# LSH attention and two gated MLPs on one core: code rows, a clamping maximum pass, bursts of value products, and single banks for the last outputs

## The chip, the cores and the metric

The kernel runs on one core of a Trainium2 chip. The metric is device microseconds of one execution, the median of several runs. Engines are named as the profile names them: PE (TensorE; PEld is its weight load), DVE (VectorE), ACT (ScalarE), POOL (GpSimd), SP (SyncE, which here only issues transfers).

## The reference

Attention of 2 batches x 8 heads, 768 positions, 64 features, in which a query sees only the keys of its own bucket; the bucket is the pattern of six signs. Two MLPs follow, 1536 tokens, width 512, inner width 2048, with outputs of their own gate each. All weights of the MLPs arrive as float64.

```python
q_bucket = sum(((q @ proj) > 0) * 2**arange(6))      # keys likewise
scores = where(q_bucket == k_bucket, q @ k.T / sqrt(64), -1e9)
attn = exp(scores - max); attn = attn / (attn.sum() + 1e-9)
x = (attn @ v) as [1536, 512]
h = x @ w_in;  x = (h - tanh(h)) @ w_out             # first MLP
h = x @ w_in2; out = (h * sigmoid(1.702 * h)) @ w_out2
```

## The kernel before

**Attention.** Heads go in eight pairs `i`. The work is a loop over 96 steps `s`: a step is 128 queries of one head against all 768 keys, twelve steps to a pair, six to a unit `u` (384 queries of both heads). In the loop, step `s` issues, in this order on PE:

- `scores(s + 2)`: two products of 128 rows each, into a score tile of two PSUM banks (tag S, two tiles). The first product has the high and low parts of q in `qa` against k doubled in `ka`; the second has q's high part and the bucket mask in `qb` against k's low part and the mask in `kb`. Rows 0 to 63 of `kb` and `qb` hold features, rows 64 to 127 the 64 buckets: a one in the key's bucket in `kb`, and -2^100 in all buckets but the query's in `qb`.
- `pv(u, c)`: one of six key chunks of the value products of the unit before, one product per head, each with half of PE's columns.
- `transposes(s)`: six 128x128 transposes of the probabilities into two banks (tag T), copied to `probT` by ACT (L377); in steps 20, 22, 44 and 46 by DVE.
- at one step of a unit, `spread`: three transposes of the inverse row sums (`rb`, L413).

`softmax` has DVE take the row maximum of the score tile (L348) and scale it (L350); ACT then takes exp from the score tile to `pr` in SBUF, with row sums (L352). The score tile comes free when exp has read it. `finish` multiplies the value products by the inverse sums (DVE) and has POOL split them into `xh` and `xl` for the MLPs.

**Preparing a pair.** `prep_ahead` runs while the pair before is worked on. At that pair's step 1 (step 3 for pair 1), POOL computes the low parts (`split_q` L238, `split_k` L244), PE the sign products (`prep_bits`, L262) and DVE their comparison with 0 (L271). At four later steps (`PO`), `prep_hot` has PE turn the bits into sums per bucket (`po`, L293), from which DVE makes the two mask blocks (L305, L308). The first scores of the new pair are issued nine steps after step 1 (seven for pair 1). The kernel does pair 0 in another way, in pieces, with ACT in it. SP's queue carries `r`, `v` and the raw weights; POOL's queue carries `ka`, `qa`, `qb`, and once `sel` (256 KB), the table of L293.

**MLPs.** 16 chunks of two inner blocks. Their work is issued in an order written by hand as a string of names (`STEADY`, and `ORDER` for single chunks): `h` and `P` are products in, `t`, `g`, `hi`, `lo` the gate and its split, `o` the products out (`out_mm`, token block t, inner block j, feature block d), `ev` the addition of the result (`evac`, L711, on DVE). A suffix - means the chunk before. Output tiles are halves of two-bank S tiles. After the last chunk an `ORDER` of its own ends the program, and each `ev` of the last chunk issues the output transfer of its block.

The scheduler is manual: the order of the code is the order on each engine, and waits are set by the tiles.

Of the kernel before, what the change touches and what calls it, by code (L numbers as in the profile page):

```python
# [57 lines left out]
def lsh_attention_then_two_mlps(  # L58
# [193 lines left out]
    def prep_bits(i, hs=(0, 1), tag="g"):  # L252
        r = heads[i][4]
        pb = ps.tile([128, 512], F32, tag=tag, name=f"pb{i}_{hs[0]}")
        if hs[0] == 0:
# [14 lines left out]
        rows = slice(hs[0] * 64, hs[-1] * 64 + 64)  # L270
        nc.vector.tensor_scalar(bits[i][rows], pb[rows, :HALF], 0.0, None, op0=ALU.is_gt)  # L271

    def prep_hot(i, h, f, tag="g"):
# [1 line left out]
        c = slice(f * HALF, (f + 1) * HALF)  # L280
# [1 line left out]
        po = ps.tile([128, 512], F32, tag=tag, name=f"po{i}_{h}_{f}")
        if i == 0:
            nc.tensor.matmul(
                po[:, :HALF],
                sel0[g : g + 32],
                bits[i][g : g + 32],
                start=True,
                stop=True,
                tile_position=(g, 0),  # L290
            )
        else:
            nc.tensor.matmul(po[:, :HALF], sel_sb[:, g // 32], bits[i], start=True, stop=True)  # L293

        def masks():
            if i == 0:
                nc.scalar.activation(
                    kb[64:128, h, c], po[64:128, :HALF], AF.Relu, bias=hot_sb[64:128], scale=BIG
                )
                nc.vector.tensor_scalar(  # L300
                    qb[64:128, h, c], po[0:64, :HALF], pop_sb[0:64], -1.0,
                    op0=ALU.subtract, op1=ALU.max,
                )
                return
            nc.vector.tensor_scalar(  # L305
                kb[64:128, h, c], po[64:128, :HALF], pop_sb[64:128], None, op0=ALU.is_equal
            )
# [51 lines left out]
    def transposes(s, on_vector):  # L359
# [5 lines left out]
        for a in range(2):  # L365
# [8 lines left out]
            if on_vector:  # L374
                copies.append((dst, src))
            else:
                nc.scalar.activation(dst, src, AF.Copy)  # L377
# [558 lines left out]
```

## Time and profile before

| | us |
|---|---|
| median of 3 runs (771.14 to 772.78) | 771.51 |
| profiled execution | 772.15 |
| its span | 770.0 |
| PE, DVE, ACT, POOL busy | 749.5, 585.1, 424.3, 400.6 |
| PE busy with `sc` (two groups), `tp`, `pv` | 55.7 + 50.2, 83.5, 82.0 |
| PE busy with `po` | 11.8 |

The span is the time between the first and the last record of the profiled execution; the rest of its own time lies around it. Busy time of PE is the union of its matmuls, which overlap, so the sum over groups is more than the union. An "idle before" names the engine whose event ended the idle time.

### The profile page before, as it was taken

To read this page: it belongs to the slowest core of one execution; us is meant where nothing else is said; L and a number is where in the kernel's file an instruction comes from. 1 tells how busy PE (TensorE), PEld (TensorE's weight loads), DVE (VectorE), ACT (ScalarE), POOL (GpSimd) and SP (SyncE) were. 2 spreads that over 40 slices of the span, in tenths; PEclk is the share of its full clock that TensorE was granted. 3 is DMA by queue.
4 is the path that set the end of the run, shared out by engine and by line. 5 is a ranking of instruction groups with operands and counts; after the bars stand their busy time and mean duration, and the time that the engine had idled before them with its cause. 6 is when DMAs were issued, how large, how long until landed. Compare 5 with 4: busy or idle time off the path is not lost.

```text
span 770.0 us, 10036 instructions
## 1 busy us (share of the span) xinstructions
PE 749.5 (97%) x3708; PEld 570.0 (74%) x3708; DVE 585.1 (76%) x840; ACT 424.3 (55%) x793; POOL 400.6 (52%) x342
## 2 busy tenths in 40 slices
PE   5899999999999999999999999999999999999996
PEld 3566666666666688888888888887888888888885
DVE  4778778767667768878887787897798778877653
ACT  3777777777778466354353543656545355353430
POOL 6451651643410586564644745699774474564620
PEclk9999999999999999999999999999999999999999
DMA  9535234043120211131112111302022211130004
GB/s 266 177 104 192 88 104 163 22 145 125 40 76 1 110 55 66 45 110 54 55 66 83 72 55 54 110 6 104 24 87 78 81 60 55 55 110 0 1 11 154
DMA packets 12993, 62.89 MB, mean 82 GB/s; under 512 B 1616, under 2 KB 2512, under 8 KB 8848
## 3 DMA queue, kind: packets, MB, share of 16 engines
q1 hardware_dynamic: 8928, 46.21, 16.7%
q0 software_dynamic: 3872, 15.99, 7.1%
q8 instruction: 29, 0.48, 0.3%
q14 instruction: 20, 0.16, 0.1%
q10 hardware_dynamic: 144, 0.05, 0.0%
HBM read 59.10 MB, written 3.15 MB: 81 GB/s over the span
## 4 chain that ended last, share of the span: by engine, by line
PE 88%; DVE 3%; POOL 2%; issue 2%; DMA 2%; ACT 1%; POOLq 0%; DVEq 0%; ACTq 0%
PE o L703 31%; PE h L614 12%; PE y L614 10%; PE pv L388 10%; PE tp L369 9%; PE sc L334 8%; PE w L614 5%; PE x L614 2%; DMA r<-in_rr 1%; DMA ka<-in_kd 1%; POOL xl L726 1%; PE rb L413 1%; PE pb L262 1%; PE po L293 1%; DVE acc L594 1%
## 5 line engine op out<-in xcount | busy, mean ns | idle before, releaser
L676 POOL TENSOR_TENSOR gl<-f,gh 128x512 fp32r<-128x512 f32 x62 | 86.2, 1390 | 162.1 <-ACT gh L671 156.7
L711 DVE TENSOR_TENSOR acc<-o,acc 128x512 f32<-128x512 f32 x168 | 108.6, 684 | 48.6 <-PE o L703 48.1
L377 ACT ACTIVATE pt<-tp 128x384 f32<-128x384 f32 x184 | 80.3, 489 | 47.9 <-PE tp L369 47.0
L348 DVE TENSOR_REDUCE nm<-sc 128x1 f32<-128x768 f32 x96 | 91.6, 954 | 14.6 <-PE sc L334 13.4
L369 PEld LDWEIGHTS tp<-eye_sb,pr 128*128 128x128 f32 x576 | 61.6, 140 | 53.5 <-issue 25.7
L145 POOL TENSOR_TENSOR wl<-w,wh 128x512 fp32r<-128x512 f32 (+1 forms) x62 | 86.4, 1405 | 19.0 <-ACT wh L142 18.9
L352 ACT ACTIVATE pr<-sc,nb 128x768 f32<-128x768 f32 x96 | 87.0, 906 | 16.0 <-DVE nb L350 8.9
L369 PE MATMUL tp<-eye_sb,pr 128*128 128x128 f32 x576 | 83.5, 281 | 0.0
L388 PE MATMUL pv<-pt,v 128*64 128x384 f32 x384 | 82.0, 510 | 0.0
L735 ACT ACTIVATE u<-y 128x512 f32<-128x512 f32 x42 | 25.2, 600 | 100.6 <-PE y L614 100.6
L703 PE MATMUL o<-wh,gh 128*128 128x512 f32 x192 | 75.0, 391 | 0.9 <-ACT acc L709 0.7
L703 PE MATMUL o<-wh,gl 128*128 128x512 f32 x192 | 74.8, 390 | 0.5 <-POOL gl L676 0.5
L703 PE MATMUL o<-gh,wh 128*128 128x512 f32 x192 | 74.8, 390 | 0.0
L703 PE MATMUL o<-wl,gh 128*128 128x512 f32 x192 | 74.7, 389 | 0.0
L703 PE MATMUL o<-gl,wh 128*128 128x512 f32 x192 | 74.7, 389 | 0.0
L703 PE MATMUL o<-gh,wl 128*128 128x512 f32 x192 | 74.7, 389 | 0.0
L614 PE MATMUL h<-xl,wh 128*128 128x512 f32 x160 | 62.4, 390 | 0.6 <-POOL xl L726 0.6
L614 PE MATMUL h<-xh,wh 128*128 128x512 f32 x160 | 62.4, 390 | 0.0
L614 PE MATMUL h<-xh,wl 128*128 128x512 f32 x160 | 62.3, 389 | 0.0
L334 PE MATMUL sc<-ka,qa 128*128 128x384 f32 x192 | 55.7, 371 | 2.3 <-DVE qa L238 1.9
L671 ACT ACTIVATE gh<-f 128x512 fp32r<-128x512 f32 x62 | 39.0, 629 | 28.7 <-DVE f L667 28.5
L334 PE MATMUL sc<-kb,qb 128*128 128x384 f32 x192 | 50.2, 342 | 2.0 <-DVE qb L300 2.0
(138 smaller groups left out, 1652.7 us busy)
## 6 DMA issues: line engine op xcount, KB each, us to landing
raw<-in_w SPq DMA_DIRECT2D x32, 1024.0 KB, 4.8
ka<-in_kd POOLq DMA_DIRECT2D x7, 768.0 KB, 4.7
qa<-in_qd POOLq DMA_DIRECT2D x7, 768.0 KB, 6.7
r<-in_rr SPq DMA_DIRECT2D x7, 768.0 KB, 4.5
v<-in_vv SPq DMA_DIRECT2D x8, 384.0 KB, 3.1
out<-acc SPq DMA_DIRECT2D x12, 256.0 KB, 2.1
qb<-in_qd POOLq DMA_DIRECT2D x7, 384.0 KB, 8.0
r<-in_rr SPq DMA_DIRECT2D x2, 384.0 KB, 4.2
```

The source lines that it names most:

```text
L145: nc.gpsimd.tensor_tensor(wl[c, j][:, f], ws[c, j][:, f], wh[c, j][:, f].bitcast(F32), ALU.subtract)
L334: nc.tensor.matmul(sc[:, hf, :HALF], (qa, qb)[n][:, h, t0 : t0 + QT], (ka, kb)[n][:, h, hf * HALF : (hf + 1) * HALF], start=(n == 0), stop ...
L348: nc.vector.tensor_reduce(nm, sc[:, :, :HALF], AX.XY, ALU.max, negate=True)
L352: nc.scalar.activation(pr.rearrange("p (a b) -> p a b", a=2), sc[:, :, :HALF], AF.Exp, bias=nb, scale=D**-0.5, accum_out=sums[u][:, j, h : ...
L369: nc.tensor.transpose(tp[:, k * 128 : (k + 1) * 128], pr[:, c * 128 : (c + 1) * 128], eye_sb)
L377: nc.scalar.activation(dst, src, AF.Copy)
L388: nc.tensor.matmul(acc[u][h * 64 : (h + 1) * 64, :UT], v[:, h, c, :], probT[u][:, c, h, :], start=(c == 0), stop=(c == NCH - 1),)
L614: nc.tensor.matmul(o, a, b, start=(start and n == 0 and m == 0), stop=(n == len(pairs) - 1 and m == 2), skip_group_check=not start,)
L671: nc.scalar.activation(gh[c, t, j], fs[c, t, j], AF.Copy)
L676: eng.tensor_tensor(gl[c, t, j], fs.pop((c, t, j)), gh[c, t, j].bitcast(F32), ALU.subtract)
L703: nc.tensor.matmul(o, a, m, start=(first and n == 0), stop=(not first and n == 2))
L711: nc.vector.tensor_tensor(m, o, m, ALU.add)
```

## The change

Four things change.

*Codes.* For pairs 1 to 7, rows 64 to 75 of `kb` and `qb` hold twelve code rows in place of 64 one-hot rows. Per head and half, `proj` is laid out so that the sign product has 24 rows: the key's six bits twice, then the query's six bits twice. DVE's comparison subtracts 1 from one copy of each (`off_sb`); POOL multiplies the key's by 2^100 (`amp_sb`, `prep_codes`); eight transfers on SP's queue (SBUF to SBUF, 12 x 384 each) bring them to their rows. The product of the two code columns is -2^100 times the number of differing bits. The second score product takes 76 rows. `po`, its masks and the `sel` load are gone for these pairs.

*Maximum pass.* Since several bits may differ, DVE's pass writes max(score, -2^100) to `pr` and puts out the row maximum as an accumulated value; exp then works on `pr` in place. The score tile comes free after DVE's pass.

*Bursts.* Value products come two chunks at a time in every second step, behind the transposes. `spread` and `gather` are one step later, `finish` comes behind `softmax`, and a unit ends one step earlier. All copies of transposes are ACT's.

*Tail.* The last chunk has an order of its own, in which the gate of its last block comes earlier and the outputs of the two inner blocks alternate per feature block; the last four output tiles lie in single banks (T, T, g, v).

```diff
+        if i == 0:
+            rows = slice(hs[0] * 64, hs[-1] * 64 + 64)
+            nc.vector.tensor_scalar(bits[i][rows], pb[rows, :HALF], 0.0, None, op0=ALU.is_gt)
+        else:
+            nc.vector.tensor_scalar(
+                bits[i], pb[:, :HALF], 0.0, off_sb, op0=ALU.is_gt, op1=ALU.subtract
+            )
+
+    def prep_codes(i):
         qa, qb, ka, kb, r = heads[i]
+        codes = sm.tile([128, HALF], F32, tag="codes", name=f"codes{i}", bufs=1)
+        nc.gpsimd.tensor_scalar_mul(codes, bits[i], amp_sb)
+        for h in range(2):
+            for f in range(2):
+                g = 64 * h + 32 * f
+                c = slice(f * HALF, (f + 1) * HALF)
+                for o, x in enumerate((kb, qb)):
+                    nc.sync.dma_start(
+                        out=x[64 : 64 + NCODE, h, c].bitcast(F32),
+                        in_=codes[g + o * NCODE : g + (o + 1) * NCODE],
+                    )
+
...
-                kb[64:128, h, c], po[64:128, :HALF], pop_sb[64:128], None, op0=ALU.is_equal
-            )
-            nc.vector.tensor_scalar(
-                qb[64:128, h, c], po[0:64, :HALF], pop_sb[0:64], -BIG,
-                op0=ALU.is_lt, op1=ALU.mult,
...
+        nb = 64 + NCODE if i else 128
...
-                    (qa, qb)[n][:, h, t0 : t0 + QT],
-                    (ka, kb)[n][:, h, hf * HALF : (hf + 1) * HALF],
+                    (qa, qb)[n][: (128, nb)[n], h, t0 : t0 + QT],
+                    (ka, kb)[n][: (128, nb)[n], h, hf * HALF : (hf + 1) * HALF],
...
-        nm = sm.tile([128, 1], F32, tag="nm", name=f"nm{s}")
-        nc.vector.tensor_reduce(nm, sc[:, :, :HALF], AX.XY, ALU.max, negate=True)
+        pr = prp.tile([128, S], F32, tag="pr", name=f"pr{s}")
+        mx = sm.tile([128, 1], F32, tag="mx", name=f"mx{s}")
+        nc.vector.tensor_scalar(
+            pr.rearrange("p (a b) -> p a b", a=2), sc[:, :, :HALF], -BIG, None,
+            op0=ALU.max, op1=ALU.max, accum_out=mx,
+        )
         nb = sm.tile([128, 1], F32, tag="nb", name=f"nb{s}")
-        nc.vector.tensor_scalar_mul(nb, nm, D**-0.5)
-        pr = prp.tile([128, S], F32, tag="pr", name=f"pr{s}")
+        nc.vector.tensor_scalar_mul(nb, mx, -(D**-0.5))
         nc.scalar.activation(
-            pr.rearrange("p (a b) -> p a b", a=2), sc[:, :, :HALF], AF.Exp,
-            bias=nb, scale=D**-0.5, accum_out=sums[u][:, j, h : h + 1],
+            pr, pr, AF.Exp, bias=nb, scale=D**-0.5, accum_out=sums[u][:, j, h : h + 1]
         )
         prob[s] = pr
...
         if k == -2:
             load_pair(i)
         elif k == 1 + first:
+            prep_bits(i)
+            prep_codes(i)
             for h in range(2):
                 split_q(i, h, nc.gpsimd)
                 split_k(i, h, nc.gpsimd)
-            prep_bits(i)
-        elif k in PO[i == 1]:
-            n = PO[i == 1].index(k)
-            prep_hot(i, n // 2, n % 2)()
         if k == 7:
             load_v(i)
...
+    bursts = {}
+    for u in range(len(pairs) * NU):
+        for c in range(NCH):
+            bursts.setdefault(2 * NQ * (u + 1) + 1 + c // 2 * 2, []).append((u, c))
+    for s in range(NSTEP + 2 * NQ + 2):
         pu, pc = divmod(s - 2 * NQ - 1, 2 * NQ)
         if s + LA < NSTEP:
             sc = scores(s + LA)
-        if pu >= 0:
-            pv(pu, pc)
-            if pc == 2 * NQ - 1:
-                finish(pu)
-        if s < NSTEP:
-            copies = transposes(s, s < 24 * CH and s % 24 in (20, 22))
-        if pu >= 0 and pc == 2:
+        copies = transposes(s, ()) if s < NSTEP else ()
+        for u, c in bursts.get(s, ()):
+            pv(u, c)
+        if pu >= 0 and pc == 3 and pu in sums:
             spread(pu)
+        late = False
+        if not late:
+            to_scalar(copies)
...
+        if True:
+            finish_all(s)
+        to_vector(copies)
+        if not True:
+            finish_all(s)
+        if pu >= 0 and pu in sums and pc == 0:
             add_eps(pu)
-        elif pu >= 0 and pc == 1:
+        if pu >= 0 and pu in sums and pc == 1:
             inverse(pu)
-        elif pu >= 0 and pc == 2:
+        if pu >= 0 and pu in sums and pc == 3:
             gather(pu)
...
-        if first and d == 0:
+        if first and d == 0 and (c, t) == (NCHUNK - 1, NTB - 1):
+            oacc[c, t] = [bank(tag, f"o{c}_{t}_{i}") for i, tag in enumerate("TTgv")]
+        elif first and d == 0:
             oacc[c, t] = [
-                ps.tile([128, 2, 512], F32, tag="S", name=f"o{c}_{t}_{i}", bufs=2)
+                o[:, i]
+                for o in (
+                    ps.tile([128, 2, 512], F32, tag="S", name=f"o{c}_{t}_{n}", bufs=2)
+                    for n in range(2)
+                )
                 for i in range(2)
             ]
...
-        o = oacc[c, t][d // 2][:, d % 2, :]
+        o = oacc[c, t][d]
...
-        NCHUNK: (
-            "ev10- ev11- ev12- ev13- g21- hi21- o200- o201- o202- o203- lo21- o210- o211- "
-            "o212- o213- ev20- ev21- ev22- ev23- "
+        NCHUNK - 1: (
+            "P1 g21- hi21- s4 shi12 ev10- ev11- P2 ev12- shi34 slo34 slo12 o200- ev13- o201- "
+            "o202- kp1 xadd o203- t00 g00 P6 lo21- P5 o210- o211- ku2 o212- o213- P7 ev21- "
+            "ev22- ku3 hi00 zadd lo00 h20 P4 ev23- t11 P3 ev20- t20 t01 g11 g20 g01 hi11 hi01 "
+            "lo11 hi20 o000 o001 wadd t10 o002 o003 lo01 h21 g10 hi10 lo20 t21 o010 lo10 g21 "
+            "hi21 o011 lo21 o012 ev00 o013 ev01 ev02 o110 o100 ev03 o111 o101 o112 o102 ev10 "
+            "o113 o103 ev11 o200 o210 ev12 ev13 o201 o211 ev20 ev21 o202 o212 ev22 o203 o213 "
+            "ev23 "
         ),
+        NCHUNK: "",
...
-    pp[0:64, 0:NBITS] = proj
-    pp[64:128, NBITS : 2 * NBITS] = proj
+    off = np.zeros((128, 1), np.float32)
+    amp = np.ones((128, 1), np.float32)
+    for n in range(2):
+        pp[0:64, n * NBITS : (n + 1) * NBITS] = proj
+        pp[64:128, NCODE + n * NBITS : NCODE + (n + 1) * NBITS] = proj
     sel = np.zeros((128, 128), np.float32)
     pop = np.zeros((128, 1), np.float32)
+    for g in range(0, 128, 32):
+        off[g : g + NBITS] = 1
+        off[g + NCODE + NBITS : g + 2 * NCODE] = 1
+        amp[g : g + NCODE] = BIG
```

On PE, around the steps 16 and 17 (`sc18` belongs to step 16, `tp16` to the same), before:

```order
L334 MATMUL sc18_623<-ka1_159,qa1_157 128x384 x2
L334 MATMUL sc18_623<-kb1_160,qb1_158 128x384 x2
L388 MATMUL pv1_532<-pt1_330,v0_111 64x384 x2
L369 MATMUL tp16_0_630<-eye_sb_92,pr16_584 128x128 x3
L369 MATMUL tp16_1_635<-eye_sb_92,pr16_584 128x128 x3
L293 MATMUL po2_0_1_647<-bits2_557,sel_sb_93 128x384
L334 MATMUL sc19_651<-ka1_159,qa1_157 128x384 x2
L334 MATMUL sc19_651<-kb1_160,qb1_158 128x384 x2
L388 MATMUL pv1_532<-pt1_330,v0_111 64x384 x2
L369 MATMUL tp17_0_658<-eye_sb_92,pr17_619 128x128 x3
L369 MATMUL tp17_1_663<-eye_sb_92,pr17_619 128x128 x3
```

and in the changed kernel:

```order
L337 MATMUL sc18_617<-ka1_157,qa1_155 128x384 x2
L337 MATMUL sc18_617<-kb1_158,qb1_156 128x384 x2
L374 MATMUL tp16_0_622<-eye_sb_92,pr16_582 128x128 x3
L374 MATMUL tp16_1_626<-eye_sb_92,pr16_582 128x128 x3
L415 MATMUL rb1_630<-eye_sb_92,wide1_590 128x128 x3
L337 MATMUL sc19_645<-ka1_157,qa1_155 128x384 x2
L337 MATMUL sc19_645<-kb1_158,qb1_156 128x384 x2
L374 MATMUL tp17_0_650<-eye_sb_92,pr17_611 128x128 x3
L374 MATMUL tp17_1_654<-eye_sb_92,pr17_611 128x128 x3
L390 MATMUL pv1_532<-pt1_330,v0_109 64x384 x4
```

The two single chunks have become one group of four products behind step 17's transposes, `po` is gone, and `rb` stands one step later than it did.

On DVE, the end of the program before (`f` is the last gate, `acc` rows are additions of output tiles, x2 for the two halves of a tile):

```order
L711 TENSOR_TENSOR acc01_71<-o15_0_0_6894,acc01_71 128x512 x2
L711 TENSOR_TENSOR acc01_71<-o15_0_1_6895,acc01_71 128x512 x2
L676 TENSOR_TENSOR gl15_1_0_6958<-w15_6815,gh15_1_0_6947 128x512
L711 TENSOR_TENSOR acc01_71<-o15_1_0_6953,acc01_71 128x512 x2
L711 TENSOR_TENSOR acc01_71<-o15_1_1_6954,acc01_71 128x512 x2
L667 TENSOR_TENSOR f15_2_1_6972<-h15_2_1_6932,f15_2_1_6972 128x512
L711 TENSOR_TENSOR acc2_2981<-o15_2_0_6994,acc2_2981 128x512 x2
L711 TENSOR_TENSOR acc2_2981<-o15_2_1_6995,acc2_2981 128x512 x2
```

and in the changed kernel:

```order
L698 TENSOR_TENSOR gl15_1_0_6894<-w15_6771,gh15_1_0_6885 128x512
L689 TENSOR_TENSOR f15_2_1_6889<-h15_2_1_6871,f15_2_1_6889 128x512
L739 TENSOR_TENSOR acc01_71<-o15_0_0_6852,acc01_71 128x512 x2
L739 TENSOR_TENSOR acc01_71<-o15_0_1_6853,acc01_71 128x512 x2
L739 TENSOR_TENSOR acc01_71<-o15_1_0_6916,acc01_71 128x512 x2
L739 TENSOR_TENSOR acc01_71<-o15_1_1_6917,acc01_71 128x512 x2
L739 TENSOR_TENSOR acc2_2937<-o15_2_0_6948,acc2_2937 128x512
L739 TENSOR_TENSOR acc2_2937<-o15_2_1_6949,acc2_2937 128x512
L739 TENSOR_TENSOR acc2_2937<-o15_2_2_6950,acc2_2937 128x512
L739 TENSOR_TENSOR acc2_2937<-o15_2_3_6951,acc2_2937 128x512
```

The last gate stands ahead of all additions now, and the last four tiles are four tiles of one bank, added one by one.

## Rows read from the trace of the kernel before

**Rows 1.** First part of the page: engine, busy us (share), instructions

```profile
PE 749.5 (97%) x3708; PEld 570.0 (74%) x3708; DVE 585.1 (76%) x840; ACT 424.3 (55%) x793; POOL 400.6 (52%) x342
```

**Rows 2.** Busy by stretch: us, then PE, PEld, DVE, ACT, POOL; clock; DMA share; GB/s

```profile
40.00:60.00 20.00, 20.00 (x126) 12.39 (x125) 16.06 (x28) 14.14 (x34) 8.80 (x6) 1.00 0.27 89
```

**Rows 3.** Timeline of PE, attention, steps with value products: start us, us, group

```profile
122.11 0.59 PE L334 MATMUL sc<-ka,qa 128*128 128x384 f32 x2
...
122.99 0.87 PE L388 MATMUL pv<-pt,v 128*64 128x384 f32 x4
123.78 0.87 PE L369 MATMUL tp<-eye_sb,pr 128*128 128x128 f32 x6
124.41 0.42 PE L293 MATMUL po<-bits,sel_sb 128*128 128x384 f32 x1
...
126.89 0.59 PE L334 MATMUL sc<-ka,qa 128*128 128x384 f32 x2
```

**Rows 4.** Timeline of PE, first steps, without value products

```profile
18.53 0.82 PE L369 MATMUL tp<-eye_sb,pr 128*128 128x128 f32 x6
19.10 0.60 PE L334 MATMUL sc<-ka,qa 128*128 128x384 f32 x2
...
19.89 0.82 PE L369 MATMUL tp<-eye_sb,pr 128*128 128x128 f32 x6
...
25.39 0.62 PE L334 MATMUL sc<-ka,qa 128*128 128x384 f32 x2
...
26.20 0.82 PE L369 MATMUL tp<-eye_sb,pr 128*128 128x128 f32 x6
```

**Rows 5.** Timeline of PE, end of the attention

```profile
249.44 0.88 PE L369 MATMUL tp<-eye_sb,pr 128*128 128x128 f32 x6
250.25 0.87 PE L388 MATMUL pv<-pt,v 128*64 128x384 f32 x4
...
251.88 2.80 PE L388 MATMUL pv<-pt,v 128*64 128x384 f32 x16
254.61 0.55 PE L413 MATMUL rb<-eye_sb,wide 128*128 128x128 f32 x3
```

**Rows 6.** Timeline of PE, waits in the attention: [idle before <-releaser]

```profile
28.97 0.41 PE L293 MATMUL po<-bits,sel_sb 128*128 128x384 f32 x1 [0.42 <-DVE qb L308]
...
29.92 0.82 PE L369 MATMUL tp<-eye_sb,pr 128*128 128x128 f32 x6
31.50 0.41 PE L293 MATMUL po<-bits,sel_sb 128*128 128x384 f32 x1 [0.77 <-DVE qb L308]
...
39.22 0.55 PE L413 MATMUL rb<-eye_sb,wide 128*128 128x128 f32 x3 [0.17 <-ACT wide L405]
...
245.82 0.62 PE L334 MATMUL sc<-ka,qa 128*128 128x384 f32 x2 [0.17 <-ACT pr L352]
```

**Rows 7.** Timeline of PE, then of DVE, the tail

```profile
762.15 0.50 PE L703 MATMUL o<-wh,gl 128*128 128x512 f32 x1 [0.48 <-POOL gl L676]
...
763.38 2.66 DVE L711 TENSOR_TENSOR acc<-o,acc 128x512 f32<-128x512 f32 x4 [3.30 <-PE o L703]
```

**Rows 8.** Groups by line: xcount | busy us, mean ns | idle before, releasers

```profile
L348 DVE TENSOR_REDUCE nm<-sc 128x1 f32<-128x768 f32 x96 | 91.6, 954 | 14.6 <-PE sc L334 13.4 <-issue 0.3
L352 ACT ACTIVATE pr<-sc,nb 128x768 f32<-128x768 f32 x96 | 87.0, 906 | 16.0 <-DVE nb L350 8.9 <-PE sc L334 6.3 <-DVE rc L403 0.4
...
L377 ACT ACTIVATE pt<-tp 128x384 f32<-128x384 f32 x184 | 80.3, 489 | 47.9 <-PE tp L369 47.0
...
L352 ACT ACTIVATION_READ_ACCUMULATOR pr<-sc,nb 128x1 f32 x96 | 19.9, 208 | 0.0
L388 PEld LDWEIGHTS pv<-pt,v 128*64 128x64 f32 x384 | 19.4, 135 | 24.5 <-issue 24.5
...
L305 DVE TENSOR_SCALAR kb<-po,tab_sb 64x384 fp32r<-64x384 f32 x28 | 17.5, 624 | 10.0 <-PE po L293 9.6
```

**Rows 9.** DMA issues, part 6 of the page: KB each, us to landing

```profile
out<-acc SPq DMA_DIRECT2D x12, 256.0 KB, 2.1
```

More of the change, by code (lines that the diff above doesn't have):

```diff
@@ L39 @@
 BIG = float(2.0**100)
-NTAB = 98
+NTAB = 100
+NCODE = 2 * NBITS
 F64_INF = float(np.uint32((1023 + 128) << 20).view(np.float32))
@@ L65, in lsh_attention_then_two_mlps @@
     tab: bass.AP,
-    sel: bass.AP,
     eye: bass.AP,
@@ L190, in lsh_attention_then_two_mlps @@
     hot_sb = tab_sb[:, 97:98]
+    off_sb = tab_sb[:, 98:99]
+    amp_sb = tab_sb[:, 99:100]
     eye_sb = cst.tile([128, 128], F32, name="eye_sb")
-    sel_sb = cst.tile([128, 4, 128], F32R, name="sel_sb")
     def pair_tiles(i):
@@ L280, in prep_hot @@
+    def prep_hot(h, f, tag="g"):
+        qa, qb, ka, kb, r = heads[0]
         c = slice(f * HALF, (f + 1) * HALF)
         g = 64 * h + 32 * f
[L282 to L290, printed above, removed]
-            )
-        else:
-            nc.tensor.matmul(po[:, :HALF], sel_sb[:, g // 32], bits[i], start=True, stop=True)
@@ L295, in masks @@
-        def masks():
[L296 to L299, printed above, removed]
-                nc.vector.tensor_scalar(
[L301 to L305, printed above, removed]
-                kb[64:128, h, c], po[64:128, :HALF], pop_sb[64:128], None, op0=ALU.is_equal
+        po = ps.tile([128, 512], F32, tag=tag, name=f"po{h}_{f}")
@@ L307, in masks @@
+        nc.tensor.matmul(
+            po[:, :HALF],
+            sel0[g : g + 32],
+            bits[0][g : g + 32],
+            start=True,
+            stop=True,
+            tile_position=(g, 0),
+        )
+        def masks():
+            nc.scalar.activation(
+                kb[64:128, h, c], po[64:128, :HALF], AF.Relu, bias=hot_sb[64:128], scale=BIG
             )
             nc.vector.tensor_scalar(
-                qb[64:128, h, c], po[0:64, :HALF], pop_sb[0:64], -BIG,
-                op0=ALU.is_lt, op1=ALU.mult,
+                qb[64:128, h, c], po[0:64, :HALF], pop_sb[0:64], -1.0,
+                op0=ALU.subtract, op1=ALU.max,
@@ L373, in transposes @@
             src = tp[:, : 3 * 128].rearrange("p (c q) -> p c q", c=3)
[L374 to L377, printed above, removed]
+            copies.append((a in on_vector, dst, src))
         return copies
@@ L449, in prep_ahead, with to_scalar, to_vector, finish_all @@
                 split_k(i, h, nc.gpsimd)
-            prep_bits(i)
-        elif k in PO[i == 1]:
-            n = PO[i == 1].index(k)
-            prep_hot(i, n // 2, n % 2)()
         if k == 7:
             load_v(i)
+    def to_scalar(copies):
+        for on_vector, dst, src in copies:
+            if not on_vector:
+                nc.scalar.activation(dst, src, AF.Copy)
+    def to_vector(copies):
+        for on_vector, dst, src in copies:
+            if on_vector:
+                nc.vector.tensor_copy(dst, src)
+    def finish_all(s):
+        for u, c in bursts.get(s, ()):
+            if c == NCH - 1:
+                finish(u)
     LA = 2
-    PO = ((2, 4, 5, 7), (4, 5, 6, 7))
     AT1 = (2, 4, 6, 8, 8, 10)
@@ L463, in lsh_attention_then_two_mlps @@
     split_k(0, 0, nc.vector)
-    masks = [prep_hot(0, 0, 0, "g"), prep_hot(0, 0, 1, "v")]
+    masks = [prep_hot(0, 0, "g"), prep_hot(0, 1, "v")]
     masks[0]()
@@ L477, in lsh_attention_then_two_mlps @@
             sc = scores(s + LA)
-        if pu >= 0:
-            pv(pu, pc)
-            if pc == 2 * NQ - 1:
-                finish(pu)
-        if s < NSTEP:
-            copies = transposes(s, s < 24 * CH and s % 24 in (20, 22))
-        if pu >= 0 and pc == 2:
+        copies = transposes(s, ()) if s < NSTEP else ()
+        for u, c in bursts.get(s, ()):
+            pv(u, c)
+        if pu >= 0 and pc == 3 and pu in sums:
             spread(pu)
+        late = False
+        if not late:
+            to_scalar(copies)
         if s + LA < NSTEP:
             softmax(s + LA, sc)
-        if s < NSTEP:
-            for dst, src in copies:
-                nc.vector.tensor_copy(dst, src)
-        if pu >= 0 and pc == 0:
+        if late:
+            to_scalar(copies)
+        if True:
[4 more added lines that the diff above has]
+        if pu >= 0 and pu in sums and pc == 0:
             add_eps(pu)
-        elif pu >= 0 and pc == 1:
+        if pu >= 0 and pu in sums and pc == 1:
             inverse(pu)
-        elif pu >= 0 and pc == 2:
+        if pu >= 0 and pu in sums and pc == 3:
             gather(pu)
@@ L705, in evac @@
     def evac(c, t, d):
-        o = oacc[c, t][d // 2][:, d % 2, :]
+        o = oacc[c, t][d]
         m = acc_of(d, t)
@@ L901 @@
                 sel[g + i, 64 + bk] = 2 * on - 1
-                sel[g + NBITS + i, bk] = 2 * on - 1
+                sel[g + NCODE + i, bk] = 2 * on - 1
     tab = np.zeros((128, NTAB), np.float32)
@@ L907 @@
     tab[:, 97:98] = BIG * (1.0 - pop)
-    sel4 = np.zeros((128, 4, 128), np.float32)
-    for g in range(4):
-        sel4[32 * g : 32 * g + 32, g] = sel[32 * g : 32 * g + 32]
+    tab[:, 98:99] = off
+    tab[:, 99:100] = amp
     arrays = {
@@ L916 @@
         "tab": tab,
-        "sel": sel4,
         "eye": np.eye(128, dtype=np.float32),
```

10 lines of the change are left out of this document (3 added, 7 removed).

## The prediction

> **What bounds the kernel now.** The page's first part comes first: PE is busy 97% of the span, DVE 76%, the others less [rows 1]. The view by stretches says the same of the attention: PE busy for all of 20 us, at a granted clock of 1.00, the 2.4 GHz level, DVE for 16 and ACT for 14 [rows 2]. So a saving counts only if it shortens what PE issues or one of PE's few waits; work taken off DVE, ACT or POOL is worth nothing by itself.
>
> The timeline of PE then prices what PE issues. I read prices from start to start of neighbouring groups, because the durations of matmuls overlap. In the attention one step is scores, value products, transposes. It lasts 2.30 us (122.11 to 124.41), and 2.48 (124.41 to 126.89) when a code matmul L293 stands ahead [rows 3]. Within the first: scores 0.88, one key chunk 0.79, transposes 0.63. Without value products the scores take 0.79 (19.10 to 19.89) or 0.81 (25.39 to 26.20, behind bit matmuls), and the transposes 0.57 (18.53 to 19.10) [rows 4]. Sixteen value matmuls in a row, four chunks, take 2.73 (251.88 to 254.61), and transposes with the next value products behind them 0.81 (249.44 to 250.25) [rows 5]. So it costs PE something to turn from full-width products to the half-width value products and back: one chunk alone takes 0.79, in a row 2.73 / 4 = 0.68, and scores and transposes are dearer beside it.
>
> PE's waits above 0.15 us in the steady attention are four: two for DVE's masks at the code matmuls (0.42, 0.77), one for ACT's `wide` and one for ACT's exp (0.17 each) [rows 6]. In the tail there is one for POOL's `gl`, 0.48, and behind the last matmul DVE still adds four output tiles [rows 7].
>
> **Part by part.**
> *Code rows instead of one-hot rows.* 28 code matmuls leave PE: 2.48 - 2.30 = 0.18 each, **-5.0 us**. The 56 masks (L305 and its twin, 0.624 us each or a little less [rows 8]) leave DVE, which gives PE nothing but the waits below. What comes instead: an offset inside the existing bit pass (nothing); one POOL pass of 128x384 ahead of four splits; per pair eight 18 KB transfers on SP's queue, ahead of `v` of the next pair and `r` of the one after. An output transfer of 256 KB takes 2.1 us to land [rows 9]; eight, even if each waited for the one before, take 17. The codes are issued some nine steps ahead of their first scores, 9 x 2.3 = 20.7 us, and `r` and `v` behind them are due a pair later. I cost this at nothing; without that cover, each of seven pairs would wait. The second score product with 76 rows streams the same 384 columns, so I take it at its present price. The `sel` load goes: 0.26 MB, at most 1 us if the start were bound by bytes; taken as 0, since the same queue then carries the next pair's loads.
>
> *Bursts.* Two steps cost 2 x 2.30 = 4.60 now. After: an even step of scores 0.81 and transposes 0.57; an odd step of scores 0.79, transposes 0.75 (0.81, less the 0.06 by which 0.63 exceeds 0.57, since no value products stand ahead of them), one chunk at 0.79 and a second in its stride at (2.73 - 0.79) / 3 = 0.65. That is 4.36, a gain of 0.24. Units 0 to 14 have three bursts each among other steps, 45 in all: **-10.8**. Unit 15's are in a row already [rows 5].
>
> *Waits that go.* Each of the four waits also costs a start from cold: at the 0.77, the group at 29.92 takes 1.58 to the next start instead of 0.57, so 1.01 is lost, 0.24 more than the bracket. Four waits: 1.53 + 4 x 0.24 = 2.5. The masks are gone, `rb` is transposed a step later, and DVE's pass frees the score tile earlier. I take 0.4 off because a step without value products is 1.36 us (0.57 + 0.79) and ACT needs more in that time: 14.14 us of 20 [rows 2], in 20 / 2.30 = 8.7 steps, 1.63 a step. **-2.1**.
>
> *The clamping pass.* It reads the tile that TENSOR_REDUCE reads in 0.954 us and also writes it; then exp reads SBUF, not PSUM [rows 8]. No row here has this pass. Bounds: 0.95 (the reduce) below, twice that above; I take the reduce, the same elements from the same tile, and add 0.2 for a separate read of the maximum, as ACT's READ_ACCUMULATOR has (0.208). DVE then has 1.85 (16.06 / 8.7) less the masks' share, plus 0.2, per step of about 2.2: covered by PE.
>
> *Copies moved to ACT.* Eight at 0.489 [rows 8], in steps where ACT converts weights too: 3.9 us, of which 0 to 3.9 may show. Two steps of ACT are 3.3 us by the window and 2 x (0.906 + 0.208 + 2 x 0.489) = 4.2 by summed rows, both under 4.36, so most is covered. I take **+1.0**.
>
> *Tail.* `gl` of the last block is made earlier: 0.48 + 0.24. Each of the last four tiles is added when its own product ends, so one addition (2.66 / 4 = 0.67) instead of two stands behind the last matmul [rows 7]. **-1.4**.
>
> The sum is -5.0 - 10.8 - 2.1 + 1.0 - 1.4 = **-18.3**. The profiled execution took 772.15 (span 770.0 and 2.15 around it); 753.85 follows. It lies 0.64 above the median of 771.51, so I forecast **753.2**.
>
> **The rivals.**
> A. *Short steps wait for ACT.* A step of 1.36 asks for two transpose banks that ACT needs 2 x 0.489 to empty, with a 0.906 exp in its order between. If the banks come 0.15 to 0.3 us late at each of 45 bursts, 6.8 to 13.5 come back: 760 to 766. For: 1.63 of ACT against 1.36. Against: the odd step lasts 3.0, and exps can run there. Chance 0.13.
>
> B. *Turning costs nothing.* If the weights of value products could be loaded under running matmuls, the gaps would have another cause and grouping saves nothing: 753.2 + 10.8 = 764. Against: the load queue shows 24.5 us of idle time ahead of the value products' weights, in which it waited for nothing in the profile [rows 8]. Chance 0.03. The Trainium skill ("TensorE: Matmul & The Clock Gate", Step-by-step: what each phase is for) has weight loads pulled ahead of matmuls in flight, where row groups do not conflict or the background buffer is the target; by that alone the change of shape would be free and rival B right. The trace speaks against it at this place.
>
> C. *DVE becomes the bound* (the slower side). If the new pass ran at half the reduce's rate, 1.91, plus 0.208 for the maximum, DVE would need per step 1.85 - 0.36 (masks, 56 x 0.62 / 96) + 1.16 = 2.65. PE's mean step now is about 2.47 (2.30, plus code, bit and `rb` work and the start). Then 96 x 0.18 = 17 more, less the tail: 787. It decides from about 1.9 for pass and read together. For: it writes 768 elements a row, the reduce one. Against: ACT's exp writes 768 elements from the same tile and sums them besides, in 0.906 [rows 8]. Chance 0.03. The Trainium skill ("VectorE: DVE Perf Modes", Two Vector instructions with no wait between them) counts an operation with an accumulator output as two instructions, the main one and an accumulator read; no DVE row here shows one, ACT's row does.
>
> D. *Codes come late.* Eight transfers behind a busy SP queue hold the first scores of a pair. At 1 us for each of seven pairs: 760; slower than before only from 2.6 us each. Against: the lead of 20 us. Chance 0.03. The Trainium skill ("DMA: Bandwidth & Descriptors", Anatomy of one DMA) gives some 2.0 us as the fixed part of a transfer; [rows 9] agrees with 2.1 for the whole.
>
> **How the numbers follow.** The forecast has 0.78, A 0.13, B, C and D 0.03 each. Low: no copy shows (-1.0), `sel` brings 1.0, ACT holds no short step (-0.4), and a short step's start gains a little more: 749.5. High: the copies show whole (+2.9) and half of A's span is taken in: 762. A measurement tells about 0.2%, 1.5 us, from no change. Slower is C, 0.03; the same 0.01; faster 0.96.
>
> **What would show it.** Right: no code matmuls; two steps taking near 4.36 from scores to scores two steps on, with the transposes in an even step followed by scores after 0.57; PE still 97% busy; the clamping pass near 0.95 us; nothing behind the code transfers; one addition after the last matmul. Wrong: PE waits on ACT `pt` or `pr` in short steps (A), an unchanged 0.79 for every chunk (B), DVE busy throughout the attention (C), scores that wait for a transfer at the start of a pair (D).

## The result, and the profile after

The changed kernel takes 752.84 us (752.62 to 752.98, four runs), the kernel before 772.0 in its company; the ratio is 0.9752, interval 0.9735 to 0.9769. The forecast was 753.2. Beside the runs below the kernel before took 771.5 to 771.9, so a difference of under half a microsecond between two kernels tells little. The profiled execution took 752.98, with a span of 751.0.

First part of the page after; it answers to [rows 1]:

```profile
PE 733.0 (98%) x3680; PEld 576.2 (77%) x3680; DVE 548.7 (73%) x872; ACT 429.4 (57%) x801; POOL 410.7 (55%) x348
```

PE lost 28 matmuls and 16.5 us and is still the bound; ACT and POOL are a little busier, DVE less.

PE's timeline of the changed kernel in the steady attention (start us, us, group), beside [rows 3]:

```profile
112.09 0.62 PE L337 MATMUL sc<-ka,qa 128*128 128x384 f32 x2
...
112.90 0.82 PE L374 MATMUL tp<-eye_sb,pr 128*128 128x128 f32 x6
113.47 0.59 PE L337 MATMUL sc<-ka,qa 128*128 128x384 f32 x2
...
114.27 0.82 PE L374 MATMUL tp<-eye_sb,pr 128*128 128x128 f32 x6
115.01 1.51 PE L390 MATMUL pv<-pt,v 128*64 128x384 f32 x8
116.45 0.62 PE L337 MATMUL sc<-ka,qa 128*128 128x384 f32 x2
```

An even step: scores 0.81, transposes 0.57. An odd one: scores 0.80, transposes 0.74, burst 1.44. Together 112.09 to 116.45, 4.36, where before two such steps took 4.60. Apart from steps that also hold sign products or `rb`, it is longer in the steady part only at steps 23 and 25, and 47 and 49, by 0.17 and 0.39 each time. Step 25, which ends with sign products and takes 4.16, has these rows:

```profile
71.24 0.59 PE L337 MATMUL sc<-ka,qa 128*128 128x384 f32 x2
71.67 0.52 PE L337 MATMUL sc<-kb,qb 76*128 76x384 f32 x2
72.32 0.93 PE L374 MATMUL tp<-eye_sb,pr 128*128 128x128 f32 x6
73.17 1.51 PE L390 MATMUL pv<-pt,v 128*64 128x384 f32 x8
```

From the second scores to the transposes 0.65 instead of 0.36, and 0.85 instead of 0.74 behind them: 0.4 late, too short and scattered to be marked as a wait. ACT's timeline tells why:

```profile
70.85 1.04 ACT L142 ACTIVATE wh<-w 128x1024 fp32r<-128x1024 f32 x1
71.80 0.84 ACT L460 ACTIVATE pt<-tp 128x384 f32<-128x384 f32 x2
```

The copies of step 24, whose transposes began at 70.67, stand behind a weight conversion.

ACT is late in two more places. At the start, where no value products stand between the short steps yet, steps 6 and 7 take 1.75 and 3.29 instead of some 1.36 and 2.97, 0.7 in all. Behind the last scores the transposes wait twice, 0.80 and 0.42 (waits of PE: us in total, times, longest):

```profile
PE tp L374 <- ACT pt L460: 1.2, 2, 0.8
```

The kernel before has no wait of this kind.

Groups by line after (xcount | busy us, mean ns | idle before, releasers), which answer to [rows 8]:

```profile
L352 DVE TENSOR_SCALAR_CACHE_REDUCE pr<-sc 128x768 f32<-128x768 f32 x96 | 91.8, 957 | 53.5 <-PE sc L337 52.3 <-ACT pt L460 0.8
...
L390 PEld LDWEIGHTS pv<-pt,v 128*64 128x64 f32 x384 | 23.5, 136 | 25.6 <-issue 25.3 <-DVE nb L357 0.3
...
L352 DVE DVE_READ_ACCUMULATOR pr<-sc 128x1 f32 x96 | 8.0, 83 | 0.0
```

The pass takes 957 ns beside the reduce's 954, and the read of the maximum 83. DVE now idles 52.3 us for PE's scores where the reduce idled 13.4.

The code transfers of pair 2, on SP's queue in the changed kernel, the first, the last, and the load behind them:

```profile
49.42 0.76 SPq L287 DMA_DIRECT2D kb<-codes  x1
...
54.93 0.71 SPq L287 DMA_DIRECT2D qb<-codes  x1
56.36 0.33 SPq L230 DMA_DIRECT2D v<-in_vv  x1
```

The first scores of that pair start at 64.99, 9.35 us after the last issue. No wait of PE names them; how long one takes to land the trace after does not tell.

### The profile page after: what moved, and what is told of

It reads as the page before. It is cut to its first block, busy times and chain, and to the rows that moved or that the text cites. A ratio compares the mean times of both kernels' runs of the same rounds, so it can differ in the third digit from the quotient of the medians.

```text
span 751.0 us, 10138 instructions
## 1 busy us (share of the span) xinstructions
PE 733.0 (98%) x3680; PEld 576.2 (77%) x3680; DVE 548.7 (73%) x872; ACT 429.4 (57%) x801; POOL 410.7 (55%) x348
## 4 chain that ended last, share of the span: by engine, by line
PE 89%; DVE 4%; ACT 2%; POOL 1%; DMA 1%; issue 1%; DVEq 0%; ACTq 0%; POOLq 0%
PE o L731 33%; PE h L636 12%; PE y L636 10%; PE sc L337 9%; PE pv L390 9%; PE tp L374 7%; PE w L636 5%; PE x L636 3%; DMA r<-in_rr 1%; POOL xl L754 1%; DVE pr L352 1%; PE pb L262 1%; ACT pr L358 1%; DVE acc L616 1%; PE rb L415 1%
## 5 line engine op out<-in xcount | busy, mean ns | idle before, releaser
L352 DVE TENSOR_SCALAR_CACHE_REDUCE pr<-sc 128x768 f32<-128x768 f32 x96 | 91.8, 957 | 53.5 <-PE sc L337 52.3
L460 ACT ACTIVATE pt<-tp 128x384 f32<-128x384 f32 x192 | 82.6, 482 | 27.6 <-PE tp L374 27.5
L358 ACT ACTIVATE pr<-pr,nb 128x768 f32<-128x768 f32 x96 | 89.8, 936 | 13.2 <-DVE nb L357 8.9
L374 PE MATMUL tp<-eye_sb,pr 128*128 128x128 f32 x576 | 79.6, 274 | 1.7 <-ACT pt L460 1.2
L374 PEld LDWEIGHTS tp<-eye_sb,pr 128*128 128x128 f32 x576 | 68.0, 140 | 8.4 <-ACT pt L460 4.6
L390 PE MATMUL pv<-pt,v 128*64 128x384 f32 x384 | 72.1, 498 | 0.0
L337 PE MATMUL sc<-ka,qa 128*128 128x384 f32 x192 | 59.1, 389 | 2.0 <-DVE qa L238 2.0
L337 PEld LDWEIGHTS sc<-ka,qa 128*128 128x128 f32 x192 | 29.5, 193 | 30.3 <-issue 22.5
L337 PE MATMUL sc<-kb,qb 76*128 76x384 f32 (+1 forms) x192 | 50.5, 344 | 2.1 <-DVE qb L310 2.1
```

What stands on the lines that cost most here:

```text
L337: nc.tensor.matmul(sc[:, hf, :HALF], (qa, qb)[n][: (128, nb)[n], h, t0 : t0 + QT], (ka, kb)[n][: (128, nb)[n], h, hf * HALF : (hf + 1) * H ...
L352: nc.vector.tensor_scalar(pr.rearrange("p (a b) -> p a b", a=2), sc[:, :, :HALF], -BIG, None, op0=ALU.max, op1=ALU.max, accum_out=mx,)
L358: nc.scalar.activation(pr, pr, AF.Exp, bias=nb, scale=D**-0.5, accum_out=sums[u][:, j, h : h + 1])
L374: nc.tensor.transpose(tp[:, k * 128 : (k + 1) * 128], pr[:, c * 128 : (c + 1) * 128], eye_sb)
L390: nc.tensor.matmul(acc[u][h * 64 : (h + 1) * 64, :UT], v[:, h, c, :], probT[u][:, c, h, :], start=(c == 0), stop=(c == NCH - 1),)
```

## The experiments

Each edit stands against the changed kernel. Twelve were run.

**One chunk at a time, behind the transposes.**

```diff
-            bursts.setdefault(2 * NQ * (u + 1) + 1 + c // 2 * 2, []).append((u, c))
+            bursts.setdefault(2 * NQ * (u + 1) + 1 + c, []).append((u, c))
```

> The changed kernel with one key chunk per step, behind the transposes, in place of bursts of two. Theory (turning PE to the half-width products and back has a price, paid once per group): per pair of steps one more turn, 0.02 at the scores + 0.18 at the transposes + 0.14 at the chunk = 0.34, 45 times, so 15.3 us more than 752.8, some 768, and 4.70 for two steps. Rival (the gain came from the other parts; grouping only brings the 0.24 of the forecast, or nothing): 10.8 more, 763.6, or 752.8.

765.89 us, ratio 0.9922 (0.9907 to 0.9937) to the kernel before: 13.05 more than the changed kernel, 0.29 per burst undone. PE's timeline:

```profile
123.23 0.62 PE L337 MATMUL sc<-ka,qa 128*128 128x384 f32 x2
...
124.04 0.82 PE L374 MATMUL tp<-eye_sb,pr 128*128 128x128 f32 x6
124.79 0.87 PE L390 MATMUL pv<-pt,v 128*64 128x384 f32 x4
125.59 0.62 PE L337 MATMUL sc<-ka,qa 128*128 128x384 f32 x2
```

A step is 2.36, two are 4.72 against 4.36. The theory's terms are all there (0.81, 0.75, 0.80), and it is these rows that decide: the time alone lies as far from the rival's 763.6 as from the theory's 768. The 15.3 is too large because a unit, `rb` included, takes 14.43 against 13.43, which makes 15 x 1.00, and because the changed kernel loses 1.1 at its four late steps and 1.2 behind the last scores, where this kernel, with its longer steps, loses 0.3 and 0.56.

**The same, ahead of the transposes**, as before the change.

```diff
-        copies = transposes(s, ()) if s < NSTEP else ()
         for u, c in bursts.get(s, ()):
             pv(u, c)
+        copies = transposes(s, ()) if s < NSTEP else ()
```

(with the edit above as well)

> The changed kernel with one key chunk per step, ahead of the transposes, as before the change. Theory (the place has a price of its own when chunks come singly: a unit takes 14.25 us ahead of the transposes in the trace of before, without code matmuls, and 14.43 behind them in a_single): 15 x 0.18 = 2.7 less than a_single's 765.9, 763.2; the four undone parts then sum to the whole gain. Rival (the place is free): 765.9.

763.40 us, ratio 0.9893 (0.9879 to 0.9908), as the theory had it. The place has a price, 2.5 us when chunks come singly; the grouping and the place together brought 763.40 - 752.84 = 10.6.

**Bursts ahead of the transposes**, by the second edit alone.

> The changed kernel with its bursts ahead of the transposes. Theory (with bursts the place is nearly free for PE): the odd step takes 0.88 + 0.79 + 0.65 + 0.63 = 2.95 against 2.98, 1.4 us less over 45, 751.4. Rival (the place behind the transposes is what gives ACT time to empty the transpose banks before the short step; ahead of them the next step's transposes wait): 0.2 to 0.5 of waiting for ACT pt at 45 places, 761 to 774.

749.91 us, ratio 0.9717 (0.9704 to 0.9730): 2.9 less than the changed kernel, the fastest version of all. PE's timeline, an even step and the odd one behind it:

```profile
109.98 0.59 PE L337 MATMUL sc<-ka,qa 128*128 128x384 f32 x2
...
110.76 0.82 PE L374 MATMUL tp<-eye_sb,pr 128*128 128x128 f32 x6
111.33 0.59 PE L337 MATMUL sc<-ka,qa 128*128 128x384 f32 x2
...
112.20 1.51 PE L390 MATMUL pv<-pt,v 128*64 128x384 f32 x8
113.64 0.88 PE L374 MATMUL tp<-eye_sb,pr 128*128 128x128 f32 x6
114.28 0.59 PE L337 MATMUL sc<-ka,qa 128*128 128x384 f32 x2
```

1.35 and 2.95: 4.30 instead of 4.36 (the theory left out the 0.03 of the even step). With `rb` a unit takes 13.27 instead of 13.43, 15 x 0.16 = 2.4. The rival has ACT's part the wrong way round: the four late steps are gone, which brings 1.1 more, for ahead of the transposes the burst, 1.44 us, gives ACT time to empty the banks. Against that, sign products now follow transposes and not value products, which costs 0.18 a pair. Grouping ahead of the transposes is worth 763.40 - 749.91 = 13.5; putting the burst behind them gave 2.9 of that back.

**Bursts of three.**

```diff
-            bursts.setdefault(2 * NQ * (u + 1) + 1 + c // 2 * 2, []).append((u, c))
+            bursts.setdefault(2 * NQ * (u + 1) + 2 + c // 3 * 3, []).append((u, c))
```

> The changed kernel with bursts of three chunks in every third step (two short steps in a row between them). Theory (turns are all that counts): one turn of 0.33 less in each of 15 units, 5 us less, 747.9. Rival (two short steps of 1.38 in a row ask more of ACT than its 1.63 a step): the transposes wait for ACT pt, 0.25 to 0.5 in 30 places, 7.5 to 15 back, 755 to 763.

752.99 us: nothing. Both theories were half right. PE's timeline, the second of two short steps and the burst step behind it:

```profile
113.09 0.59 PE L337 MATMUL sc<-ka,qa 128*128 128x384 f32 x2
...
114.45 0.60 PE L337 MATMUL sc<-ka,qa 128*128 128x384 f32 x2
114.89 0.52 PE L337 MATMUL sc<-kb,qb 76*128 76x384 f32 x2
115.51 0.93 PE L374 MATMUL tp<-eye_sb,pr 128*128 128x128 f32 x6
116.36 2.16 PE L390 MATMUL pv<-pt,v 128*64 128x384 f32 x12
118.45 0.62 PE L337 MATMUL sc<-ka,qa 128*128 128x384 f32 x2
```

This burst step takes 4.00; the other one of a unit takes 3.62. The transposes start 0.62 behind the second scores instead of 0.36. Such a unit takes 13.44 as in the changed kernel (13.43): the turn saved, 0.37, is lost to late transposes. It is so in eight of the 15 units. In six others sign products stand between the two short steps, and the burst step takes 3.65; but transposes followed by sign products take 0.75 instead of 0.57. And at the steps 23 and 47 the transposes wait 0.70 for ACT.

**Relief for ACT by DVE.** Copies of the steps 22, 24, 46 and 48 go to DVE in the first; in the others, with bursts of three, also the second copy of every step that is a multiple of 6, behind DVE's pass or (the last) ahead of it.

```diff
-        copies = transposes(s, ()) if s < NSTEP else ()
+        copies = transposes(s, (0, 1) if s in (22, 24, 46, 48) else ()) if s < NSTEP else ()
```

> The changed kernel with the copies of steps 22, 24, 46 and 48 on DVE again (8 of them, at other steps than before the change). Theory (the copies moved to ACT show where ACT also converts weights: steps 23 and 25, 47 and 49 of the changed kernel take 0.17 and 0.39 longer than their like): 1.1 us less, 751.7. Rival (DVE's copies come behind its pass and hold the banks as long): 752.8 or more.

> As a_three, with the second copy of the first short step of each unit's run on DVE, behind its pass, and the copies of steps 22, 24, 46 and 48 there too. Theory (in a_three the turn saved, 0.37 a unit, is given back as 0.38 of waiting for ACT pt in the second burst step): with ACT relieved by 0.48 that wait goes, 15 x 0.38 + 1.1 = 6.8 less than a_three, some 746. Rival (DVE's pass then comes late by its copy, or the bank is held as long): 753.

> As a_three_dve, with DVE's copies ahead of its pass. Theory: the bank is free earlier than in a_three_dve, 746 or a little less. Rival (the pass, and behind it exp and the transposes two steps on, come late by the copy and its wait for the transposes): 753 to 758.

753.86, 756.35 and 762.31 us: 1.0, 3.5 and 9.5 more than the changed kernel. All three theories fell. The rivals hold in kind, but the second and third version cost more than theirs (753, and 753 to 758); and the 15 waits that the second theory wanted to win back are eight. In the first the late steps grew (4.51 for step 25 instead of 4.16). The waits of PE in the three kernels, one row each (engine, line, waited for: us in total, times, longest):

```profile
PE tp L374 <- ACT wh L142: 1.0, 2, 0.5
```

```profile
PE tp L374 <- DVE pt L465: 2.3, 4, 0.7
```

```profile
PE tp L374 <- ACT pt L460: 8.3, 16, 0.8
```

In the second the bank is free only when DVE, behind its pass, has copied it: the second short step takes 1.69 instead of 1.36, and the burst step gets back 3.67. In the third the pass comes late, and with it ACT: the burst step takes 4.63. In the first, DVE's timeline at step 22 shows what else stands in the queue:

```profile
67.13 1.01 DVE L465 COPY pt<-tp 128x384 f32<-128x384 f32 x2
68.06 0.55 DVE L423 COPY rbs<-rb 128x384 f32<-128x384 f32 x1
68.52 1.22 DVE L136 SCALAR_TENSOR_TENSOR w<-raw,w 128x1024 f32<-128x1024 f32 x1
69.66 0.95 DVE L352 TENSOR_SCALAR_CACHE_REDUCE pr<-sc 128x768 f32<-128x768 f32 x1
```

The copies push `rbs` and the weight work back by 1.0, and the pass with them (69.66, in the changed kernel 68.67). The exp behind it waits 1.63 for its `nb` instead of 0.36, `wh` and the copies behind that come later still.

**One-hot rows again.** `prep_bits`, `prep_hot`, `sel` and the 128 rows of before, with

```diff
+    PO = ((2, 3, 5, 7), (4, 5, 6, 7))
```

> The changed kernel with the one-hot rows of before (28 code matmuls, 56 masks, the sel load, 128 rows), the code matmuls in the steps 2, 3, 5 and 7 of a pair. Theory (only PE's 28 code matmuls counted, and the two waits for masks): 28 x 0.18 = 5.0 and up to 1.7 for the waits, 757.8 to 759.5. Rival (the masks kept DVE so busy that its pass came late in the short steps): 28 pairs of masks of 1.23 us, of which 0.25 to 0.5 shows each, so 7 to 14 on top, 765 to 772.

760.27 us, ratio 0.9850 (0.9835 to 0.9864): 7.4 more, 0.8 above the theory's range and 5 below the rival's. The two waits for masks are back, in PE's timeline of this kernel, about as long together as in [rows 6]:

```profile
28.42 0.42 PE L293 MATMUL po<-bits,sel_sb 128*128 128x384 f32 x1 [0.53 <-DVE qb L308]
...
30.89 0.41 PE L293 MATMUL po<-bits,sel_sb 128*128 128x384 f32 x1 [0.69 <-DVE qb L308]
```

A step with a code matmul takes 0.2 to 0.3 more than its like, but the scores behind it take 0.1 less, which leaves the 0.17 or so of the theory. What the theory lacks stands at `rb`, which starts 0.90 behind the start of its transposes instead of 0.65, in six pairs. PE and DVE of this kernel, then PE of the changed one:

```profile
53.90 0.82 PE L371 MATMUL tp<-eye_sb,pr 128*128 128x128 f32 x6
54.80 0.52 PE L412 MATMUL rb<-eye_sb,wide 128*128 128x128 f32 x3
```

```profile
54.04 0.61 DVE L308 TENSOR_SCALAR qb<-po,tab_sb 64x384 fp32r<-64x384 f32 x1
```

```profile
52.38 0.82 PE L374 MATMUL tp<-eye_sb,pr 128*128 128x128 f32 x6
53.03 0.49 PE L415 MATMUL rb<-eye_sb,wide 128*128 128x128 f32 x3
```

`po` and `rb` lie in the same bank (tag g), and DVE reads it for the second mask until 54.65; the trace marks no wait, but bank and times fit. These 6 x 0.25 = 1.5 us come from undoing the codes alone, with `rb` a step later and the code matmuls in other steps than before, so they are no price of the code matmuls. A pass of DVE that comes late for a short step, as the rival has it, does not show.

**Reduce and exp from the score tile.** The lines of `softmax` before, in place of the pass; the clamp is left out.

> The changed kernel with DVE's TENSOR_REDUCE and exp from the score tile, as before, so that the clamp at -2^100 is left out (rows with no key in the bucket come out differently). Theory (the pass costs what the reduce costs, and the score tile is early enough either way): 0 to 0.4 us more, 752.8 to 753.3. Rival (in bursts the short steps of 1.38 need the score tile before exp has read it): 0.2 to 0.5 us of waiting for ACT pr at the scores in each of 45 short steps, 762 to 775.

752.78 us: the same, as the theory had it. The short steps do not wait for exp beyond two places at the start (waits of PE):

```profile
PE sc L337 <- ACT pr L355: 0.6, 2, 0.3
```

**The old tail.**

```diff
-        if first and d == 0 and (c, t) == (NCHUNK - 1, NTB - 1):
-            oacc[c, t] = [bank(tag, f"o{c}_{t}_{i}") for i, tag in enumerate("TTgv")]
-        elif first and d == 0:
+        if first and d == 0:
```

(and the `ORDER` of before)

> The changed kernel with the end of the program of before (order, two-bank tiles). Theory (the sum of the forecast: the wait for gl 0.72 and one addition 0.67): 1.4 us more, 754.2. Rival (behind the last matmul the output transfers of a pair of tiles also queue, which the spacing of the changed kernel avoids): 1.58 behind the last matmul and 0.72 for gl, 2.3 more, 755.1.

754.41 us, ratio 0.9773 (0.9757 to 0.9789): 1.57 more, nearer the theory. From the start of the last matmul to the end the old tail takes 752.5 - 747.70 = 4.80, the new one 751.0 - 746.91 = 4.09:

```profile
745.49 0.50 PE L729 MATMUL o<-wh,gl 128*128 128x512 f32 x1 [0.48 <-POOL gl L698]
...
747.70 0.40 PE L729 MATMUL o<-wh,gl 128*128 128x512 f32 x1
```

```profile
746.91 0.39 PE L731 MATMUL o<-wh,gl 128*128 128x512 f32 x1
```

(the old tail's kernel first, with its wait for `gl`). 0.71 is one addition, as forecast. The rival's 1.58 came from the one profile of the kernel before, whose end was 0.9 longer with the same tail (770.0 - 764.33 = 5.67).

**Full-width value products**, single and in bursts.

```diff
-                acc[u][h * 64 : (h + 1) * 64, :UT],
-                v[:, h, c, :],
+                acc[u][:, :UT],
+                v[:, h, min(c, 4) : min(c, 4) + 2].rearrange("p c d -> p (c d)"),
```

> As a_single, with value products of the full 128x128 shape (two chunks of v as weights, so the attention's values are not the reference's). Theory (it is the half-width shape that makes PE's turns dear): chunks at 4 x 0.22 = 0.88, scores 0.79 and transposes 0.57 with nothing lost between, 2 x 2.24 = 4.48 for two steps, about 759, and within 1 us of f_burst. Rival (any change from one group of products to another costs the same): 13 us above f_burst, as a_single is above the changed kernel.

> As the changed kernel, with value products of the full 128x128 shape (the attention's values are not the reference's). Theory (half-width shape): no gain from bursts, 4.48 for two steps, 48 x 0.12 = 6 us more than the changed kernel, some 759, the same as f_single. Rival (any change of group costs): 13 us below f_single.

(The products of both heads add into one block of sums here, so the edit changes more than the width.)

799.28 and 797.70 us. Grouping brings 1.6 here, not 13, as the theory had it; but both are 39 to 40 us above what it expected. PE's timeline, single first, then burst:

```profile
132.60 1.46 PE L390 MATMUL pv<-pt,v 128*128 128x384 f32 x4
133.60 0.81 PE L337 MATMUL sc<-ka,qa 128*128 128x384 f32 x2
134.24 0.52 PE L337 MATMUL sc<-kb,qb 76*128 76x384 f32 x2
```

```profile
131.91 2.75 PE L390 MATMUL pv<-pt,v 128*128 128x384 f32 x8
134.19 0.80 PE L337 MATMUL sc<-ka,qa 128*128 128x384 f32 x2
134.83 0.51 PE L337 MATMUL sc<-kb,qb 76*128 76x384 f32 x2
```

A row of matmuls ends with the end of its last one, and one lasts 0.49 (mean 486 to 487 ns in both kernels). So in a row of four they start (1.46 - 0.49) / 3 = 0.32 apart, and in a row of eight (2.75 - 0.49) / 7 = 0.32: the price of one is the same. From start to start the rows take 1.00 and 2.28 only because the scores behind them start 0.02 to 0.03 after the last matmul's start; they give it back, with 0.64 to the second scores instead of 0.43.

That explains the 39 to 40 us: the expectations have 0.22 for a matmul, for which no row here speaks, and 96 chunks x 4 x 0.10 is 38. And it bears the theory out. If turning cost nothing, two steps would take 8 x 0.32 + 2 x (0.79 + 0.57) = 5.3. Singly they take 133.60 to 138.90, 5.30, and in bursts 130.47 to 135.76, 5.29. So a turn to full-width value products and back costs nothing that can be seen, and a turn to half-width ones 0.3 us. It is the half-width shape, or the two heads in two halves of the columns that come with it, that makes PE's turns dear; what PE does in such a turn stays open. Two half-width matmuls start together (in the changed kernel at 115.71 and 115.72, then at 116.03 and 116.04), so two of them cost what one full-width matmul does.

## Why the prediction was right

| part | forecast | measured by undoing it |
|---|---|---|
| bursts and their place; copies on ACT | -10.8, +1.0, +0.4 for ACT's short steps | -10.6 (to single chunks ahead of the transposes, copies left on ACT) |
| code rows, with their two mask waits | -5.0, -1.7 | -7.4, of which some 1.5 are `rb`'s |
| clamping pass, with the wait for exp | 0, -0.4 | +0.1 |
| `spread` a step later (wait for `wide`) | -0.4 | not undone |
| tail | -1.4 | -1.6 |
| sum | -18.3 | -19.5 |

(The 2.5 of the forecast's waits is split here: two for masks, 0.66 and 1.01, two for ACT, 0.41 each.) The four measured parts add to 19.5 where the whole moved 19.2. That says less than it seems: without `rb`'s wait, which the undoing itself brought in, they add to 18.0, and no run puts the copies back on DVE at the steps of before, or `spread` and `finish` in their old places.

*Bound and price.* Starts read from start to start gave 4.36 for two steps, and it is 4.36. That number came from rows of the kernel before in which each group already stood beside the neighbour it would get: transposes without value products ahead, value products behind transposes, products in a row. Busy times of the groups, which overlap, would not have given it: a chunk is busy for 0.87 where it takes 0.79.

*Bursts.* The forecast costed the grouping and the place as one. They have opposite signs: grouping in the old place brings 13.5, the place behind the transposes costs 2.9. The forecast's sum used 0.75 for transposes followed by value products (measured: 0.74), so it held the loss without naming it; the same rows, 0.88 + 1.44 + 0.63 + 1.36 = 4.31, would have said that ahead is better.

*Copies moved to ACT.* At first sight +1.0 has the right size; the four late steps lose twice 0.17 + 0.39 = 1.1 in the trace. Only the step behind 22, with 0.17, follows a copy that was moved; the 0.39 stands behind copies of step 24, which were ACT's before too, and comes from the weight conversion ahead of them in a step that has become short. So the cause in that term was named half right. The copies were not put back at the very steps of before in a run. And ACT's lateness is more than that: with 0.7 in steps 6 and 7 and 1.2 behind the last scores it comes to 3.0, where the forecast has 1.0 and 0.4.

*What evens it out* stood in no term. Sign products now follow value products; in the kernel before they followed transposes, which then took 0.80 instead of 0.63, so six pairs gain 0.17 each, 1.0 in all. And a unit became 0.75 shorter (13.43, from 14.18 with single chunks ahead of the transposes), not 3 x 0.24 = 0.72, which is 0.5 more over 15. That the total came out within 1 us is thus partly luck; that the bursts, the codes and the tail made it, with the prices read from the rows, is not.

*Codes.* The price per code matmul holds, 0.17 for 0.18, and the second scores start the same 0.35 to 0.36 ahead of the next group with 76 rows as with 128. The undo costs 0.7 more than the sum, and `rb`'s wait is more than that. The cover held with room: eight transfers take 6.2 us to issue one behind the other, and POOL's splits, which end at 57.02, come after them.

*Rival A* was real in kind: ACT's banks are late in the four steps, in steps 6 and 7 and behind the last scores, 3.0 us, not in 45 places and 6.8 to 13.5. Bursts of three show how near it was, since two short steps in a row without other work between them are enough to lose all that a turn saves. *Rival B* falls with single chunks: 13.05 and 13.5. With full-width products it would have been right. The Trainium skill ("TensorE: Matmul & The Clock Gate", Step-by-step: what each phase is for) has weight loads pulled ahead of running matmuls; here that does not make the turns to half-width products free. But the evidence that the forecast gave against B was poor: the load queue's idle time ahead of the value products' weights is 25.6 us after the change [rows 8: 24.5], with half as many groups. It is no measure of the price of a turn. *Rival C* needed 1.9 us for pass and read; they take 1.04. The Trainium skill ("VectorE: DVE Perf Modes", Two Vector instructions with no wait between them) counts pass and accumulator read as two instructions, and the trace after shows them as two, 957 and 83 ns. *Rival D*: no wait for a code transfer. The 2.0 us quoted there from the Trainium skill ("DMA: Bandwidth & Descriptors", Anatomy of one DMA) is in that section a figure for transfers that POOL issues; the code transfers are issued from SP's queue, and no run here shows the fixed part of one.

## What to carry to other kernels

Where one engine issues without pause, price a reordering from start to start of groups, and look for each pair of neighbours in the trace; price the place and the size of a group apart, since one can eat part of the other. Look also at how the group behind starts: the last matmul of a row can hide under it, and a short row then looks cheaper per matmul than it is. The place of a group also sets how long other engines have: value products ahead of the transposes gave ACT time that behind them it lacked. When the fast part of a loop is shortened, ask which other engine's turn-round it now falls below: two steps below ACT's time in a row, with nothing between them, cost as much as the turn they saved. Moving a copy to an engine with idle time helps only if that engine is idle at that moment: here all three tries cost time.

Bursts of two ahead of the transposes, 749.91 us, beat both kernels.

## What was not expected of the hardware

A transfer of 12 rows of 1.5 KB within SBUF takes SP's queue 0.71 us to issue (median of the 56; the longest 1.15), that of a 384 KB load 0.33; eight in a row hold the queue for 6.2 us. DVE's read of an accumulated value takes 83 ns, ACT's 191. Full-width value matmuls start 0.32 us apart whether four or eight stand in a row, and turning to them costs nothing that can be seen; half-width ones run two at a time at the same 0.32 (0.79 us for a single chunk of four, 1.44 for eight), and each turn to them costs 0.3 us.
